# Layer-norm scalings set apart from their GpSimd rsqrt batches in a fused spectral-filter and GEGLU kernel

## The chip, the cores and the metric

The kernel runs on one core of one Trainium2 chip. The metric is the device time of one execution in microseconds (us), and the kernel before takes 195.79 us (median of three runs, 195.38 to 196.23). Engine names in the profile lines are PE (TensorE, matrix products), PEld (TensorE's weight loads), DVE (VectorE), ACT (ScalarE), POOL (GpSimd) and SP (SyncE). "Granted clock" is the share of TensorE's full clock that the throttle let through, 1.00 at best.

Executions over 1.5% slower than the fastest of the same kernel are left out of the means. Medians and ranges are over all executions.

## The reference

The input x is one batch of 2048 rows of 512 bf16 values. The output is x, plus a spectral filter of the layer-normed rows, plus a GEGLU feed-forward of the same layer-normed rows.

```python
def reference(A_x, A_w_r, A_w_i, B_x, B_w_gate, B_w_up, B_w_down):
    # A: y = irfft2(rfft2(x) * (w_r + i w_i)) over rows and features
    # B: y = (gelu(x @ w_gate) * (x @ w_up)) @ w_down, inner width 1792
    x = A_x
    xn = _layernorm(x, axis=-1)        # (x - mean) / sqrt(var + 1e-5), per row
    return x + _A_ref(xn, A_w_r, A_w_i) + _B_ref(xn, B_w_gate, B_w_up, B_w_down)
```

## The kernel before

The 2048 rows lie as 16 "columns" of 128 partitions by 512 features. Columns 0 to 3 are normalised on VectorE at the very start. Columns 4 to 15 are normalised in three groups of four:

```python
def layernorm(c0, n):                       # c0 = 4, 8, 12 with n = 4
    V = nc.vector
    ...
    for j in range(n):                      # mean and variance on VectorE
        tc.keep_in_program_order(V.bn_stats(out=stats[:, j, :], in_=x_t[:, c0 + j, :]))
        V.bn_aggr(out=mv[:, j, :], in_=stats[:, j, :])
    rsqrt(V if c0 < 4 else nc.gpsimd, rstd, mv[:, :, 1], n)   # 14 GpSimd operations, 3 Newton steps
    if c0 >= 4:
        nb = pw.tile([P, n], F32, name="nb")                  # 2 more
        nc.gpsimd.tensor_tensor(out=nb[:], in0=mv[:, :, 0], in1=rstd[:], op=ALU.mult)
        nc.gpsimd.tensor_scalar(out=nb[:], in0=nb[:], scalar1=-1.0, scalar2=None, op0=ALU.mult)
    for j in range(n):
        if c0 < 4: ...
        else:                               # the "scaling": xn = x * rstd + nb, on ScalarE
            nc.scalar.activation(out=xn[:, c0 + j, :], in_=x_t[:, c0 + j, :], func=AF.Identity,
                                 bias=nb[:, j:j + 1], scale=rstd[:, j:j + 1])
```

After that each column is transposed by a DMA (tile xnT, for the GEGLU matmuls), and VectorE folds it (tiles A and xf, for the spectral part). Four short matmul groups for each fold give PSUM tiles bp, which ScalarE copies to Bs. When all of Bs is there, the first dp matmuls can start. That is the line that divides the first third of the kernel, which this study is about, from the rest.

The GEGLU part consists of 69 blocks. One block is eight matmuls, then a GELU on ScalarE, then a multiply on VectorE:

```python
gp = ps.tile([P, w], F32, name="g_ps", tag="G", bufs=2)    # two PSUM buffers each
up = ps.tile([P, w], F32, name="u_ps", tag="U", bufs=2)
for e in range(NE): nc.tensor.matmul(gp[:], lhsT=Wg_sb..., rhs=rhs[:, e, :], ...)
for e in range(NE): nc.tensor.matmul(up[:], lhsT=Wu_sb..., rhs=rhs[:, e, :], ...)
ge = pw.tile([P, w], BF16, name="ge", bufs=3)
nc.scalar.activation(out=ge[:], in_=gp[:], func=AF.Gelu_apprx_tanh)
nc.vector.tensor_tensor(out=hT[sb, fc][:, o:o + w], in0=up[:], in1=ge[:], op=ALU.mult)
```

A list of tasks with a time each says where among the blocks the other work is issued. (The list counts up by 1.724 for each GEGLU block of 512 rows, so a unit is a bit more than half a block.)

```python
tasks = [(20, load_tables), (28, gather_tables)]
for cg in range(1, 4):
    t = 7 + 6 * (cg - 1)
    tasks.append((t, lambda cg=cg: layernorm(4 * cg, 4)))
    tasks.append((t + 6, lambda cg=cg: transposes(4 * cg, 4)))
for cg in range(4):
    t = 8 + 7 * cg
    tasks.append((t, lambda cg=cg: fold(cg)))
    for q in range(4):
        tasks.append((t + 3 + q, lambda cg=cg, q=q: pstep(cg, q)))   # bp matmuls and the Bs copy
tasks.append((36, tables_fix))
```

gather_tables issues six indirect DMAs from GpSimd.

## Time and profile before

| reading | value | view |
|---|---|---|
| time | 195.79 us, span of the profiled run 193.6 us | times, page |
| TensorE busy | 174.2 us, 90% | page, part 1 |
| TensorE idle between 17 and 64 us | 8.84 us, nearly all in three gaps | table by stretch, TensorE timeline |
| ScalarE's waits for GpSimd between 17 and 66 us | 8.9 us in three waits | waits of ScalarE |

The page of the kernel before: the busy time of each engine, and in 40 slices of the span the busy tenths of TensorE and its granted clock in tenths.

```profile
PE 174.2 (90%) x1080; PEld 93.2 (48%) x1080; DVE 116.4 (60%) x273; ACT 97.8 (51%) x181; POOL 18.8 (10%) x68
...
PE   0699975996929999999999999999999999999992
...
PEclk9999996999996999999999999999999999999999
```

TensorE is the engine at its limit. It dips in slices 6 and 7, 10 and 12 (a slice is 4.84 us), and its clock dips in slices 7 and 13. TensorE's timeline of the kernel before shows where they lie. The columns are start, busy time, engine, line, operation, tiles, shapes, count, and in brackets the idle time before and what ended it.

```profile
31.31 1.86 PE L475 MATMUL g_ps<-xnT_70,Wg_sb 128*128 128x512 bf16 x4 [3.55 <-ACT ge L481]
...
45.62 1.89 PE L475 MATMUL g_ps<-xnT_71,Wg_sb 128*128 128x512 bf16 x8 [1.56 <-ACT ge L481]
...
57.26 0.40 PE L331 MATMUL bp<-RF_t,xf 128*128 128x128 bf16 x4 [3.57 <-ACT Bs L337]
```

Each gap is ended by ScalarE: by a GELU (ge) or by a Bs copy that frees the PSUM buffer TensorE wants. ScalarE's timeline of the kernel before says why these came late.

```profile
28.07 2.93 ACT L269 ACTIVATE xn<-x_t,nb,rstd 128x512 bf16<-128x512 bf16 x4 [3.37 <-POOL nb L262]
30.90 0.36 ACT L481 ACTIVATE ge<-g_ps 128x256 bf16<-128x256 f32 x1
...
41.69 2.93 ACT L269 ACTIVATE xn<-x_t,nb,rstd 128x512 bf16<-128x512 bf16 x4 [1.42 <-POOL nb L262]
...
52.22 2.93 ACT L269 ACTIVATE xn<-x_t,nb,rstd 128x512 bf16<-128x512 bf16 x4 [4.08 <-POOL nb L262]
```

ScalarE takes its instructions in order. It stands at the first scaling with nothing to do for 3.37 us, then runs four scalings as a block of 2.93 us, and only then reaches the GELU at 30.90 that TensorE has been waiting for. What it stands waiting for is the rsqrt on GpSimd, 16 operations in a row. Part of the third of these batches, GpSimd's timeline of the kernel before:

```profile
46.77 0.23 POOL L235 TENSOR_SCALAR v<-mv 128x4 f32<-128x4 f32 x1 [5.12 <-DVE mv L257]
...
47.36 1.17 POOL L239 TENSOR_TENSOR t<-rstd 128x4 f32<-128x4 f32 x1
...
51.96 0.23 POOL L262 TENSOR_SCALAR nb<-nb 128x4 f32<-128x4 f32 x1
```

Last, the table by stretch of the kernel before. Its columns are the stretch, its length, then busy time and count of PE, PEld, DVE, ACT and POOL, the granted clock, the DMA share and GB/s.

```profile
31.30:34.40 3.10, 3.09 (x9) 1.11 (x9) 3.10 (x7) 1.99 (x4) 0.00 (x0) 0.56 0.80 130
...
57.30:61.50 4.20, 4.20 (x21) 2.16 (x22) 2.21 (x4) 1.97 (x5) 1.97 (x2) 0.59 1.14 233
61.50:134.60 73.10, 73.10 (x442) 37.17 (x439) 53.61 (x123) 56.86 (x103) 2.03 (x10) 1.00 0.23 63
```

After the first and the third gap the clock is about half (0.56, 0.59), so those two gaps cost more than their own length. From 61.5 us on TensorE is busy all the time at full clock.

### The profile page before, as it was taken

What the parts mean: (1) busy time and instruction counts of PE and PEld (TensorE: products, weight loads), DVE (VectorE), ACT (ScalarE), POOL (GpSimd) and SP (SyncE); (2) the same over time, 40 slices, a digit from 0 to 9 for tenths busy, and PEclk for the clock granted to TensorE, in tenths of its full rate; (3) what the DMA queues carried; (4) which work ended last, traced back from release to release, by engine and by line L of the source; (5) the groups of instructions that cost most, each with busy time, mean ns of one, the idle gap of its engine ahead of it and who ended that gap; (6) DMA issues with size and microseconds to landing.
All of it is one profiled execution on the core that took longest, in us unless ns stands there. A gap on an engine that the chain in (4) does not pass through costs nothing.

```text
span 193.6 us, 3075 instructions
## 1 busy us (share of the span) xinstructions
PE 174.2 (90%) x1080; PEld 93.2 (48%) x1080; DVE 116.4 (60%) x273; ACT 97.8 (51%) x181; POOL 18.8 (10%) x68
## 2 busy tenths in 40 slices
PE   0699975996929999999999999999999999999992
PEld 0688841542504544555554554545444444444440
DVE  2779915967453439868977897963726425434521
ACT  2443528377295588688898888546312112121100
POOL 0000050243774200000000000000000000000000
PEclk9999996999996999999999999999999999999999
DMA  5999914405089300220229322020021322222210
GB/s 151 326 386 387 312 48 99 68 0 108 0 216 167 110 0 0 54 51 8 54 57 327 109 56 54 3 54 0 18 67 56 108 72 77 71 81 81 68 67 28
DMA packets 22064, 19.38 MB, mean 100 GB/s; under 512 B 8289, under 2 KB 20577, under 8 KB 22049
## 3 DMA queue, kind: packets, MB, share of 16 engines
q1 hardware_dynamic: 20816, 17.22, 31.1%
q0 software_dynamic: 416, 1.32, 2.8%
q10 hardware_dynamic: 816, 0.66, 1.1%
q8 instruction: 8, 0.13, 0.3%
q14 instruction: 8, 0.06, 0.1%
HBM read 13.41 MB, written 2.10 MB: 80 GB/s over the span
## 4 chain that ended last, share of the span: by engine, by line
PE 71%; issue 7%; DVE 6%; POOL 6%; DMA 5%; ACT 3%; SPq 0%; DVEq 0%; ACTq 0%; POOLq 0%
PE y_ps L488 25%; PE u_ps L478 18%; PE g_ps L475 17%; DMA Wu_sb<-in_B_w_up_dram 4%; ACT xn L269 2%; DVE stats L256 2%; PE yp L443 2%; PE gp L428 2%; PE dp L344 2%; PE y_ps L490 2%; PE ep L356 2%; DVE hT_154 L482 2%; DMA x_t<-in_A_x_dram 2%; POOL t L239 1%; POOL rstd L248 1%
## 5 line engine op out<-in xcount | busy, mean ns | idle before, releaser
L481 ACT ACTIVATE ge<-g_ps 128x512 bf16<-128x512 f32 (+2 forms) x69 | 35.3, 520 | 22.1 <-PE g_ps L475 20.8
L478 PEld LDWEIGHTS <-Wu_sb 128*128 128x128 bf16 x276 | 26.7, 102 | 24.8 <-issue 2.6
L475 PEld LDWEIGHTS <-Wg_sb 128*128 128x128 bf16 x276 | 25.6, 101 | 24.5 <-issue 7.0
L493 DVE TENSOR_TENSOR y_sb<-y_ps,y_sb 128x512 bf16<-128x512 f32 x16 | 11.1, 692 | 30.2 <-PE y_ps L490 30.2
L449 ACT CAST yf<-yp 128x512 bf16<-128x512 f32 x16 | 9.2, 587 | 37.3 <-PE yp L443 37.3
L475 PE MATMUL g_ps<-xnT_70,Wg_sb 128*128 128x256 bf16 (+2 forms) x108 | 18.6, 297 | 4.2 <-ACT ge L481 3.6
L359 ACT CAST E<-ep 64x512 bf16<-64x512 f32 x32 | 18.5, 579 | 4.2 <-PE ep L356 3.9
L478 PE MATMUL u_ps<-xnT_70,Wu_sb 128*128 128x256 bf16 (+2 forms) x108 | 17.9, 292 | 0.4 <-DMA Wu_sb<-in_B_w_up_dram 0.3
L475 PE MATMUL g_ps<-xnT_71,Wg_sb 128*128 128x512 bf16 x56 | 14.7, 390 | 1.6 <-ACT ge L481 1.6
L478 PE MATMUL u_ps<-xnT_71,Wu_sb 128*128 128x512 bf16 x56 | 15.4, 397 | 0.0
L478 PE MATMUL u_ps<-xnT_72,Wu_sb 128*128 128x512 bf16 x56 | 14.4, 379 | 0.0
L478 PE MATMUL u_ps<-xnT_73,Wu_sb 128*128 128x512 bf16 x56 | 14.4, 379 | 0.0
L475 PE MATMUL g_ps<-xnT_73,Wg_sb 128*128 128x512 bf16 x56 | 14.4, 379 | 0.0
L475 PE MATMUL g_ps<-xnT_72,Wg_sb 128*128 128x512 bf16 x56 | 14.4, 379 | 0.0
L482 DVE TENSOR_TENSOR hT_687<-u_ps,ge 128x512 bf16<-128x512 f32 x14 | 9.5, 688 | 8.2 <-PE u_ps L478 5.5
L482 DVE TENSOR_TENSOR hT_154<-u_ps,ge 128x256 bf16<-128x256 f32 (+2 forms) x27 | 11.4, 426 | 3.4 <-PE u_ps L478 2.7
L269 ACT ACTIVATE xn<-x_t,nb,rstd 128x512 bf16<-128x512 bf16 x12 | 8.8, 801 | 8.9 <-POOL nb L262 8.9
L488 PE MATMUL y_ps<-Wd_sb,hT_1030 128*128 128x512 bf16 x56 | 12.7, 379 | 0.0
L488 PE MATMUL y_ps<-Wd_sb,hT_154 128*128 128x512 bf16 x56 | 12.7, 379 | 0.0
L488 PE MATMUL y_ps<-Wd_sb,hT_687 128*128 128x512 bf16 x56 | 12.7, 379 | 0.0
L337 ACT CAST Bs<-bp 128x512 bf16<-128x512 f32 x16 | 8.8, 582 | 2.9 <-PE bp L331 2.9
L337 ACT CAST ds<-dp 128x512 bf16<-128x512 f32 x16 | 9.2, 606 | 1.8 <-PE dp L344 1.8
(133 smaller groups left out, 223.4 us busy)
## 6 DMA issues: line engine op xcount, KB each, us to landing
y_sb<-in_A_x_dram SPq DMA_DIRECT2D x16, 128.0 KB, 2.1
out_dram<-y_sb SPq DMA_DIRECT2D x16, 128.0 KB, 1.7
Wd_sb<-in_B_w_down_dram SPq DMA_DIRECT2D x1, 1792.0 KB, 9.3
x_t<-in_A_x_dram SPq DMA_DIRECT2D x3, 512.0 KB, 12.4
Wg_sb<-in_B_w_gate_dram SPq DMA_DIRECT2D x1, 768.0 KB, 9.1
Wu_sb<-in_B_w_up_dram SPq DMA_DIRECT2D x1, 768.0 KB, 10.8
Wg_sb<-in_B_w_gate_dram SPq DMA_DIRECT2D x2, 256.0 KB, 5.3
Wg_sb<-in_B_w_gate_dram SPq DMA_DIRECT2D x1, 512.0 KB, 6.1
```

The lines of the kernel that those rows point to most:

```text
L256: tc.keep_in_program_order(V.bn_stats(out=stats[:, j, :], in_=x_t[:, c0 + j, :]))
L269: nc.scalar.activation(out=xn[:, c0 + j, :], in_=x_t[:, c0 + j, :], func=AF.Identity, bias=nb[:, j:j + 1], scale=rstd[:, j:j + 1])
L337: nc.scalar.copy(out=o, in_=i)
L344: nc.tensor.matmul(dp[:, q // 2, q % 2, :], lhsT=Bs[:, q, G].rearrange("p c r a -> p (c r a)"), rhs=FQ[q], start=(q == 0), stop=(q == 3), ...
L359: nc.scalar.copy(out=E[64 * h:64 * h + 64, r], in_=ep[64 * r:64 * r + 64])
L449: nc.scalar.copy(out=yf[:, c % 2], in_=yp[:])
L475: nc.tensor.matmul(gp[:], lhsT=Wg_sb[:, e, fc * P:(fc + 1) * P], rhs=rhs[:, e, :], start=(e == 0), stop=(e == NE - 1))
L478: nc.tensor.matmul(up[:], lhsT=Wu_sb[:, e, fc * P:(fc + 1) * P], rhs=rhs[:, e, :], start=(e == 0), stop=(e == NE - 1))
L481: nc.scalar.activation(out=ge[:], in_=gp[:], func=AF.Gelu_apprx_tanh)
L482: nc.vector.tensor_tensor(out=hT[sb, fc][:, o:o + w], in0=up[:], in1=ge[:], op=ALU.mult)
L488: nc.tensor.matmul(y_ps[:], lhsT=hT[sb, f][:, cl * P:(cl + 1) * P], rhs=Wd_sb[:, f, :], start=(f == 0), stop=False)
L493: nc.vector.tensor_tensor(out=y_sb[:], in0=y_ps[:], in1=y_sb[:], op=ALU.add)
```

## The change

The intent is that ScalarE should never stand before a scaling whose rsqrt isn't finished, and should never have four scalings in one block. The moments (mean and variance) are computed column by column, the eight last columns share one rsqrt batch, and each scaling is its own task, kept in program order, one or two per GEGLU block, about three blocks after the rsqrt is issued. Folds and short matmuls move to suit. Renamings in rsqrt and in the code of the first two columns are cut from the diff.

```diff
-    def layernorm(c0, n):
+    mv = pc.tile([P, NC, nc.vector.BN_AGGR_DIM], F32, name="mv")     # one tile for all columns
+    rstd = pc.tile([P, NC], F32, name="rstd")
+    nb = pc.tile([P, NC], F32, name="nb")
+
+    def moments(c):
         V = nc.vector
         ...
-        for j in range(n):
-            tc.keep_in_program_order(V.bn_stats(out=stats[:, j, :], in_=x_t[:, c0 + j, :]))
-            V.bn_aggr(out=mv[:, j, :], in_=stats[:, j, :])
-        rsqrt(V if c0 < 4 else nc.gpsimd, rstd, mv[:, :, 1], n)
+        tc.keep_in_program_order(V.bn_stats(out=stats[:], in_=x_t[:, c, :]))
+        V.bn_aggr(out=mv[:, c, :], in_=stats[:])
+
+    def scales(V, c0, n):
+        r, b = rstd[:, c0:c0 + n], nb[:, c0:c0 + n]
+        rsqrt(V, r, mv[:, c0:c0 + n, 1], n)
         if c0 >= 4:
             ... (nb = -mean * rstd, as before)
-        for j in range(n):
-            ...
-                nc.scalar.activation(out=xn[:, c0 + j, :], in_=x_t[:, c0 + j, :], func=AF.Identity,
-                                     bias=nb[:, j:j + 1], scale=rstd[:, j:j + 1])
+
+    def normalize(c):
+        ...
+            tc.keep_in_program_order(
+                nc.scalar.activation(out=xn[:, c, :], in_=x_t[:, c, :], func=AF.Identity,
+                                     bias=nb[:, c:c + 1], scale=rstd[:, c:c + 1]))
@@ tasks
-    for cg in range(1, 4):
-        t = 7 + 6 * (cg - 1)
-        tasks.append((t, lambda cg=cg: layernorm(4 * cg, 4)))
-        tasks.append((t + 6, lambda cg=cg: transposes(4 * cg, 4)))
+    for c0, n, t in ((4, 4, 8), (8, 8, 14)):
+        for c in range(c0, c0 + n):
+            j = c - c0
+            tasks.append((t + 0.8 * j, lambda c=c: moments(c)))
+            tasks.append((t + n + 5 + 0.9 * j, lambda c=c: (normalize(c), transposes(c, 1))))
+        tasks.append((t + n - 0.5, lambda c0=c0, n=n: scales(nc.gpsimd, c0, n)))
     for cg in range(4):
-        t = 8 + 7 * cg
+        t = (8, 21, 30.5, 34)[cg]
         tasks.append((t, lambda cg=cg: fold(cg)))
         for q in range(4):
-            tasks.append((t + 3 + q, lambda cg=cg, q=q: pstep(cg, q)))
+            tasks.append((t + (3 + q if cg < 2 else 1.5 + 0.6 * q), lambda cg=cg, q=q: pstep(cg, q)))
```

More of the change, by code (lines that the diff above doesn't have):

```diff
@@ L231, in rsqrt @@
     def rsqrt(V, y, var, n):
-        v = pw.tile([P, n], F32, name="v")
-        t = pw.tile([P, n], F32, name="t")
+        v = pc.tile([P, n], F32, name=f"v{n}")
+        t = pc.tile([P, n], F32, name=f"t{n}")
         V.tensor_scalar(out=v[:], in0=var, scalar1=EPS, scalar2=None, op0=ALU.add)
-        vi, yi = v[:].bitcast(I32), y[:].bitcast(I32)
+        vi, yi = v[:].bitcast(I32), y.bitcast(I32)
         V.tensor_scalar(out=yi, in0=vi, scalar1=-0.5, scalar2=float(0x5F3759DF), op0=ALU.mult, op1=ALU.add)
         for _ in range(3):
-            V.tensor_tensor(out=t[:], in0=y[:], in1=y[:], op=ALU.mult)
+            V.tensor_tensor(out=t[:], in0=y, in1=y, op=ALU.mult)
             if V is nc.vector:
@@ L242, in rsqrt @@
                                        op0=ALU.mult, op1=ALU.mult)
-                V.scalar_tensor_tensor(out=y[:], in0=t[:], scalar=1.5, in1=y[:],
+                V.scalar_tensor_tensor(out=y, in0=t[:], scalar=1.5, in1=y,
                                        op0=ALU.add, op1=ALU.mult)
@@ L247, in rsqrt @@
             V.tensor_scalar(out=t[:], in0=t[:], scalar1=-0.5, scalar2=1.5, op0=ALU.mult, op1=ALU.add)
-            V.tensor_tensor(out=y[:], in0=t[:], in1=y[:], op=ALU.mult)
-    def layernorm(c0, n):
-        V = nc.vector
-        stats = pw.tile([P, n, V.BN_STATS_DIM], F32, name="stats")
-        mv = pw.tile([P, n, V.BN_AGGR_DIM], F32, name="mv")
-        rstd = pw.tile([P, n], F32, name="rstd")
-        for j in range(n):
-            tc.keep_in_program_order(V.bn_stats(out=stats[:, j, :], in_=x_t[:, c0 + j, :]))
-            V.bn_aggr(out=mv[:, j, :], in_=stats[:, j, :])
-        rsqrt(V if c0 < 4 else nc.gpsimd, rstd, mv[:, :, 1], n)
-        if c0 >= 4:
-            nb = pw.tile([P, n], F32, name="nb")
-            nc.gpsimd.tensor_tensor(out=nb[:], in0=mv[:, :, 0], in1=rstd[:], op=ALU.mult)
-            nc.gpsimd.tensor_scalar(out=nb[:], in0=nb[:], scalar1=-1.0, scalar2=None, op0=ALU.mult)
-        for j in range(n):
-            if c0 < 4:
-                V.tensor_scalar(out=xn[:, c0 + j, :], in0=x_t[:, c0 + j, :],
-                                scalar1=mv[:, j, 0:1], scalar2=rstd[:, j:j + 1],
-                                op0=ALU.subtract, op1=ALU.mult)
-            else:
-                nc.scalar.activation(out=xn[:, c0 + j, :], in_=x_t[:, c0 + j, :], func=AF.Identity,
-                                     bias=nb[:, j:j + 1], scale=rstd[:, j:j + 1])
@@ new lines, in rsqrt @@
+            V.tensor_tensor(out=y, in0=t[:], in1=y, op=ALU.mult)
+    mv = pc.tile([P, NC, nc.vector.BN_AGGR_DIM], F32, name="mv")
+    rstd = pc.tile([P, NC], F32, name="rstd")
+    nb = pc.tile([P, NC], F32, name="nb")
+    def moments(c):
+        V = nc.vector
+        stats = pw.tile([P, V.BN_STATS_DIM], F32, name="stats")
+        tc.keep_in_program_order(V.bn_stats(out=stats[:], in_=x_t[:, c, :]))
[3 more added lines that the diff above has]
+        rsqrt(V, r, mv[:, c0:c0 + n, 1], n)
+        if c0 >= 4:
+            V.tensor_tensor(out=b, in0=mv[:, c0:c0 + n, 0], in1=r, op=ALU.mult)
+            V.tensor_scalar(out=b, in0=b, scalar1=-1.0, scalar2=None, op0=ALU.mult)
@@ L272, in first_columns @@
+    def normalize(c):
+        if c < 4:
+            nc.vector.tensor_scalar(out=xn[:, c, :], in0=x_t[:, c, :], scalar1=mv[:, c, 0:1],
+                                    scalar2=rstd[:, c:c + 1], op0=ALU.subtract, op1=ALU.mult)
+        else:
+            tc.keep_in_program_order(
+                nc.scalar.activation(out=xn[:, c, :], in_=x_t[:, c, :], func=AF.Identity,
+                                     bias=nb[:, c:c + 1], scale=rstd[:, c:c + 1]))
     def first_columns():
         V = nc.vector
-        stats = pw.tile([P, 2, V.BN_STATS_DIM], F32, name="stats")
@@ L276, in first_columns @@
-        mv = pw.tile([P, 2, V.BN_AGGR_DIM], F32, name="mv")
-        rstd = pw.tile([P, 2], F32, name="rstd")
+        stats = pc.tile([P, 2, V.BN_STATS_DIM], F32, name="stats2")
         def step(k, c):
@@ L497 @@
     first_columns()
-    layernorm(2, 2)
+    for c in (2, 3):
+        moments(c)
+    scales(nc.vector, 2, 2)
+    for c in (2, 3):
+        normalize(c)
     transposes(2, 2)
```

## The prediction

> **What bounds the kernel now.** TensorE. From 61.5 us to 190 us the table of engine busy time by stretch shows it busy all the time at granted clock 1.00. All its idle time after 17 us lies in three gaps (TensorE timeline): 3.55 us up to 31.3, 1.56 us up to 45.6, 3.57 us up to 57.3. Each has the same shape (timelines of GpSimd and ScalarE): the 16 GpSimd operations of a four-column rsqrt take 4.2 to 5.2 us (23.6-27.8, 37.2-41.4, 46.8-52.0), while ScalarE, which runs in order, already stands before the four scalings that wait for it and then runs them as one block of 2.93 us (28.1, 41.7, 52.2). The GELUs or Bs copies behind the block hold the PSUM buffers that TensorE needs. ScalarE idles 3.4, 1.4 and 4.1 us before the blocks.
>
> The two gaps over 3.5 us also cost clock: 0.56 granted in 31.3-34.4, 0.59 in 57.3-61.5; after the 1.56 us gap it stayed 1.00. The Trainium skill, "TensorE: Matmul & The Clock Gate", Part 1, says that about 3.4 us of idleness halves the clock, and this trace agrees. Eight 512-wide matmuls at 0.216 us need 1.73 us and took 3.07: 1.3 us lost; in the last stretch 2.39 us of matmuls took 4.2: 1.8 us. Total recoverable: 8.7 + 3.1, about 11.8 us.
>
> **What the change does.** Matmuls, GELUs and the 12 scalings (0.80 us) stay. One of three GpSimd batches goes, about 4.4 us (another becomes 8 wide, at 0.21 us an operation by the trace's 128x8 ones). More important is the order: the moments of columns 8-15 move up to the end of the first GEGLU quarter, and each scaling batch starts about one GpSimd batch (4.7 us) after its moments. In the built order of ScalarE the scalings stand one or two behind each GELU (after blocks 23, 24, 24, 25; then 29 to 33), no longer in fours. Folds and short matmuls move to suit.
>
> **Walk with the trace's durations (estimates).** Batch one again starts at 23.6, ends at 28.0; ScalarE reaches its first scaling at 29.2: no wait. Last scaling 33.7, last transpose (1.25 us issue, 2.5 to landing) about 36.5; TensorE wants it at 36.2: 0.4 us stall. Batch two: 33.8 to 38.5, stretched up to 2 us where VectorE's folds run beside it (before, one GpSimd operation took 1.17 us beside them instead of 0.20); ScalarE wants it at 40.6: 0 to 0.5. From there ScalarE is nearly saturated until the last scaling at 51.4; the folds follow it closely, so the short matmuls stall 0.5 us (columns 8-11) and 0.3 us (12-15), and the first dp matmuls wait about 1 us for the Bs copies. New stalls together 2 to 2.5 us, none long enough to cost clock. Before, the GEGLU block behind the first dp ended at 69.2; after, at about 59. From there the order is the same and TensorE-bound, so the gain stays in the total.
>
> **Prediction: 185.8 us, 184.0 to 189.5**; faster by over 2% 0.94, within 2% 0.05, slower 0.01.
>
> **Signs.** TensorE idle 17-62 us falls from 8.7 to 1.5-3 us; granted clock near 1.00 from 17 us on; ScalarE's waits for GpSimd vanish; no ScalarE block of 2.93 us; tail from the first dp on unchanged.
>
> **What would make it wrong.** A scaling that still reaches ScalarE's head before batch two is done; late transposes at the second quarter; folds pinned before GEGLU multiplies on VectorE; the gathers crowding the transposes' DMA.

## The result

The changed kernel takes 185.48 us (median of four runs, 185.20 to 185.55), beside 195.58 us for the kernel before in the same rounds. The ratio is 0.948, with a 95% interval of 0.945 to 0.951. All ratios here are the mean time of one kernel's fast runs over that of the other's of the same rounds, so they are not quite the ratio of the medians that are quoted.

The same lines of the page, for the changed kernel:

```profile
PE 172.2 (94%) x1080; PEld 92.7 (50%) x1080; DVE 116.1 (63%) x273; ACT 97.8 (53%) x181; POOL 17.2 (9%) x52
...
PE   0699999899899999999999999999999999999991
...
PEclk9999999999999999999999999999999999999998
```

The dips are gone, of TensorE as of its clock (all but the last slice). TensorE's timeline of the changed kernel has two stalls left between 17 and 64 us, both short:

```profile
36.72 1.02 PE L477 MATMUL g_ps<-xnT,Wg_sb 128*128 128x512 bf16 x4 [0.55 <-DMA xnT<-xn]
...
48.96 0.40 PE L333 MATMUL bp<-RF_t,xf 128*128 128x128 bf16 x4 [0.60 <-DVE xf L323]
```

The first waits for a transposing DMA, the second for a fold. TensorE's whole idle time there, read from the table by stretch as 47.00 us less its busy time, is 1.19 us (45.81 busy), where it was 8.84 us (38.16 busy). ScalarE's waits between 17 and 66 us, first the kernel before, then the changed one (columns: engine, waiting tile and line, what it waited for, us in total, times, longest us):

```profile
ACT xn L269 <- POOL nb L262: 8.9, 3, 4.1
```

```profile
ACT xn L273 <- POOL nb L265: 0.4, 1, 0.4
```

8.9 us have become 0.4 us. On ScalarE's timeline of the changed kernel no scalings stand in blocks of four. The first of each batch:

```profile
28.97 0.81 ACT L273 ACTIVATE xn<-x_t,nb,rstd 128x512 bf16<-128x512 bf16 x1
...
42.00 0.81 ACT L273 ACTIVATE xn<-x_t,nb,rstd 128x512 bf16<-128x512 bf16 x1 [0.37 <-POOL nb L265]
```

The eight-wide batch on GpSimd took 5.8 us, from 36.16 to 41.97. GpSimd's timeline of the changed kernel:

```profile
36.16 0.60 POOL L235 TENSOR_SCALAR v<-mv 128x8 f32<-128x8 f32 x1 [7.22 <-DVE mv L258]
...
37.40 0.20 POOL L239 TENSOR_TENSOR t<-rstd 128x8 f32<-128x8 f32 x1
...
38.59 0.52 POOL L248 TENSOR_TENSOR rstd<-t,rstd 128x8 f32<-128x8 f32 x1
...
41.73 0.24 POOL L265 TENSOR_SCALAR nb<-nb 128x8 f32<-128x8 f32 x1
```

And VectorE's timeline of the changed kernel beside it:

```profile
36.56 0.68 DVE L321 TENSOR_TENSOR A<-xn 128x1024 bf16<-128x1024 bf16 x1
37.17 0.69 DVE L484 TENSOR_TENSOR hT<-u_ps,ge 128x512 bf16<-128x512 f32 x1
...
38.37 0.68 DVE L325 TENSOR_TENSOR xf<-A 128x1024 bf16<-128x1024 bf16 x1
```

Four of the sixteen GpSimd operations took 0.48 to 0.60 us instead of 0.20. They are those that meet a fold (tiles A and xf, both inputs in SBUF), and not those that meet a GEGLU multiply (hT, which reads one input from PSUM), such as the one at 37.40. The Trainium skill, "SBUF — State Buffer", section "Who interferes with whom", says that VectorE and GpSimd share a port pair as an exclusive lock, and that a tensor_tensor with both inputs in SBUF contends with GpSimd's reads. This trace agrees: each of the four ends about 0.1 us after the end of the fold that it met.

The time can be followed along the kernel. The first dp matmul starts at 56.24 us instead of 66.86 (10.6 us earlier). The addition of the last output on VectorE starts at 179.82 instead of 190.01 (10.2 us), and the span ends 9.8 us earlier. So nearly everything that was gained in the first third stayed gained. The half microsecond that went missing behind was not followed up.

### The profile page after: what moved, and what is told of

Read it like the earlier page. It is cut to its first block, busy times and chain, and to the rows that moved or that the text cites. A ratio compares the mean times of both kernels' runs of the same rounds, so it can differ in the third digit from the quotient of the medians.

```text
span 183.8 us, 3059 instructions
## 1 busy us (share of the span) xinstructions
PE 172.2 (94%) x1080; PEld 92.7 (50%) x1080; DVE 116.1 (63%) x273; ACT 97.8 (53%) x181; POOL 17.2 (9%) x52
## 4 chain that ended last, share of the span: by engine, by line
PE 83%; DVE 4%; DMA 3%; POOL 3%; issue 3%; ACT 2%; ACTq 0%
PE y_ps L490 26%; PE g_ps L477 22%; PE u_ps L480 22%; DMA Wu_sb<-in_B_w_up_dram 3%; PE dp L346 2%; PE ep L358 2%; PE yp L445 2%; PE gp L430 2%; PE y_ps L492 2%; DVE hT L484 2%; PE bp L333 2%; ACT xn L273 1%; ACT ge L483 1%; DVE stats L257 1%; PE tp L306 1%
## 5 line engine op out<-in xcount | busy, mean ns | idle before, releaser
L477 PE MATMUL g_ps<-xnT,Wg_sb 128*128 128x512 bf16 (+2 forms) x276 | 62.3, 347 | 1.1 <-DMA xnT<-xn 0.5
L480 PE MATMUL u_ps<-xnT,Wu_sb 128*128 128x512 bf16 (+2 forms) x276 | 60.9, 344 | 0.1
L490 PE MATMUL y_ps<-Wd_sb,hT 128*128 128x512 bf16 x224 | 51.0, 379 | 0.0
L484 DVE TENSOR_TENSOR hT<-u_ps,ge 128x512 bf16<-128x512 f32 (+2 forms) x69 | 40.1, 583 | 15.0 <-PE u_ps L480 7.5
L490 PEld LDWEIGHTS <-hT 128*128 128x128 bf16 x224 | 21.3, 98 | 23.1
L339 ACT CAST Gs<-gp 128x512 bf16<-128x512 f32 x16 | 8.6, 591 | 1.4 <-PE gp L430 1.4
L257 DVE BATCH_NORM_STATS2 stats<-x_t 128x6 f32<-128x512 bf16 x14 | 9.2, 667 | 0.0
L492 PE MATMUL y_ps<-yt,RI_t 128*128 128x512 bf16 x16 | 6.1, 379 | 0.0
L346 PE MATMUL dp<-CT,Bs 128*128 128x128 bf16 x64 | 6.0, 219 | 0.0
L333 PE MATMUL bp<-RF_t,xf 128*128 128x128 bf16 x64 | 5.4, 219 | 0.6 <-DVE xf L323 0.6
## 6 DMA issues: line engine op xcount, KB each, us to landing
Wu_sb<-in_B_w_up_dram SPq DMA_DIRECT2D x1, 768.0 KB, 10.6
```

Of the source, the lines that this page charges most:

```text
L257: tc.keep_in_program_order(V.bn_stats(out=stats[:], in_=x_t[:, c, :]))
L339: nc.scalar.copy(out=o, in_=i)
L346: nc.tensor.matmul(dp[:, q // 2, q % 2, :], lhsT=Bs[:, q, G].rearrange("p c r a -> p (c r a)"), rhs=FQ[q], start=(q == 0), stop=(q == 3), ...
L477: nc.tensor.matmul(gp[:], lhsT=Wg_sb[:, e, fc * P:(fc + 1) * P], rhs=rhs[:, e, :], start=(e == 0), stop=(e == NE - 1))
L480: nc.tensor.matmul(up[:], lhsT=Wu_sb[:, e, fc * P:(fc + 1) * P], rhs=rhs[:, e, :], start=(e == 0), stop=(e == NE - 1))
L490: nc.tensor.matmul(y_ps[:], lhsT=hT[sb, f][:, cl * P:(cl + 1) * P], rhs=Wd_sb[:, f, :], start=(f == 0), stop=False)
```

## The experiments

Three explanations can be given for the gain. They are called A, B and C in the expectations:

- A, distance: the scalings reach ScalarE's head after their rsqrt is done, so ScalarE no longer stands idle.
- B, fewer batches: one of three GpSimd batches is gone.
- C, splitting: there is no longer a block of four scalings (2.93 us) in front of the GELUs.

The first four kernels ran on one chip, where the kernel before took 195.59 us (194.67 to 196.48, seven runs). The other eight ran on another chip, where it took 195.48 and 195.37 us.

### Distance alone: d_delay_only

This is the kernel before with its three batches of four and its blocks of four scalings. Only the scalings are issued later (kept in program order), with the transposes; folds and short matmuls move as far as that needs.

```diff
-        for j in range(n):
-            ... the four scalings, right after the rsqrt
+    def scalings(cg):                      # the same four, in program order
+        ...
-        tasks.append((t + 6, lambda cg=cg: transposes(4 * cg, 4)))
+        tasks.append(((0, 17, 24, 29)[cg], lambda cg=cg: (scalings(cg), transposes(4 * cg, 4))))
     for cg in range(4):
-        t = 8 + 7 * cg
+        t = (8, 21, 28, 34)[cg]
         ...
-            tasks.append((t + 3 + q, lambda cg=cg, q=q: pstep(cg, q)))
+            tasks.append((t + (3 + q if cg < 3 else 1.5 + 0.6 * q), lambda cg=cg, q=q: pstep(cg, q)))
```

> Kernel before with one thing changed: the four ScalarE scalings of a batch are issued one GpSimd batch later (three batches of 4, scalings still in blocks of four, moments as before; folds and short matmuls moved behind them as they must). Theory A, the gain is the distance between a batch and its scalings: no wait of ScalarE for GpSimd over 0.5 us, no TensorE gap over 1.5 us, 185 to 187.5 us. Rival B, the gain is the GpSimd batch that went: 191 us or more. Rival C, the gain is that the scalings no longer stand in a block of 2.93 us: 190 us or more.

Measured: 185.51 us (185.42 to 185.63), ratio 0.948, 95% 0.944 to 0.952. That is the ratio of the whole change. ScalarE's timeline of this kernel, and then its TensorE timeline:

```profile
29.13 2.92 ACT L276 ACTIVATE xn<-x_t,nb,rstd 128x512 bf16<-128x512 bf16 x4
...
36.04 2.92 ACT L276 ACTIVATE xn<-x_t,nb,rstd 128x512 bf16<-128x512 bf16 x4
...
45.29 2.93 ACT L276 ACTIVATE xn<-x_t,nb,rstd 128x512 bf16<-128x512 bf16 x4 [2.66 <-POOL nb L262]
```

```profile
36.60 1.02 PE L482 MATMUL g_ps<-xnT,Wg_sb 128*128 128x512 bf16 x4 [0.23 <-DMA xnT<-xn]
...
48.75 1.02 PE L482 MATMUL g_ps<-xnT,Wg_sb 128*128 128x512 bf16 x4 [1.99 <-ACT ge L488]
```

Two blocks of 2.92 us came with no wait before them, and no GELU gap on TensorE followed: the stall at 36.60 is a transposing DMA's. The third block came 2.66 us before its rsqrt was done and cost a gap of 1.99 us. So a block by itself is harmless; a block with a wait before it is not. Two signs that A expected (no wait over 0.5 us, no gap over 1.5 us) thus failed for the third block, though the time came as expected. B and C fall as explanations of the gain, and A stands. No run moves the folds and short matmuls alone, so their share in this version isn't shown; b_first_batch_no_distance below moves scalings and transposes alone.

### Three batches instead of two: a_three_batches

This is the changed kernel with the eight-wide batch split into two of four.

```diff
-        tasks.append((t + n - 0.5, lambda c0=c0, n=n: scales(nc.gpsimd, c0, n)))
+        for h in range(c0, c0 + n, 4):
+            tasks.append((t + 0.8 * (h - c0 + 3) + 0.1 if h + 4 < c0 + n else t + n - 0.5,
+                          lambda h=h: scales(nc.gpsimd, h, 4)))
```

> Changed kernel with its 8-column rsqrt batch cut into two of 4 (48 GpSimd operations again instead of 32), everything else at the same places. A: 185.0 to 185.8 us, since the added 4.5 us of GpSimd stay behind ScalarE's other work. B: 4 us longer, about 189.5 us.

Measured: 186.13 us (185.88 to 186.32), ratio 0.951, 95% 0.947 to 0.955. It is 0.3 us above what A expected and 3.4 us below what B expected. ScalarE waits nowhere for GpSimd. The 0.3 us are not the batches' doing as far as the trace shows: TensorE's timeline has one gap more than expected, 1.07 us at 54.41, which is of the kind found further below (late releases). B falls a second time.

### Blocks of four scalings: c_blocks_of_four

This is the changed kernel with its scalings in blocks of four again, at the time of the first of each four.

```diff
-            tasks.append((t + n + 5 + 0.9 * j, lambda c=c: (normalize(c), transposes(c, 1))))
+            tasks.append((t + n + 5 + 3.6 * (j // 4), lambda c=c: (normalize(c), transposes(c, 1))))
```

> Changed kernel with the scalings again in blocks of four, at the delayed time of the first of each four. A: a block of 2.93 us that waits for nothing fits between the GELUs of two buffers, TensorE idles at most 1.5 us in all, 185 to 187 us. C: the block itself holds up the GELUs, gaps of about 3 us come back, 190 us or more.

Measured: 187.85 us (187.60 to 188.44), ratio 0.960, 95% 0.956 to 0.965. That lies above what A expected (185 to 187) and below what C expected (190 or more). ScalarE's timeline of this kernel, then its TensorE timeline, then its table by stretch:

```profile
28.90 2.93 ACT L273 ACTIVATE xn<-x_t,nb,rstd 128x512 bf16<-128x512 bf16 x4
...
42.92 2.93 ACT L273 ACTIVATE xn<-x_t,nb,rstd 128x512 bf16<-128x512 bf16 x4 [1.63 <-POOL nb L265]
```

```profile
46.86 1.90 PE L477 MATMUL g_ps<-xnT,Wg_sb 128*128 128x512 bf16 x5 [2.52 <-ACT ge L483]
```

```profile
43.88:47.29 3.41, 0.89 (x5) 0.29 (x3) 1.41 (x3) 3.41 (x7) 2.50 (x4) 1.00 0.65 166
47.29:50.71 3.42, 3.42 (x10) 1.21 (x9) 2.90 (x5) 3.30 (x6) 2.59 (x3) 0.50 1.08 209
```

The first block, which had no wait, again caused no gap. The second waited 1.63 us for the eight-wide batch and caused a gap of 2.52 us, the only one. The clock then halved for 3.42 us, in which TensorE was busy all the time: a loss of about 1.7 us by this trace (half of 3.42). The times show less: one of the four executions ran at clock 1.00 throughout and took 187.60 us, where the other three (clock 0.986 to 0.991) took 187.84 to 188.44. The prediction's reading, that it takes about 3.4 us of idleness, doesn't foresee this half-clock stretch. So a block matters where its batch is late. Whether single scalings would have made less of the same wait isn't shown: in the changed kernel the wait at this place was only 0.37 us.

This table also tells how the clock is judged. The windows are 3.41 us long and lie on a fixed grid. Narrowing the stretches of this table finds the two half-clock stretches of the kernel before at 30.65 to 34.06 and 57.95 to 61.36, which is 27.30 us or 8 steps of 3.41 us apart. The table by stretch of the kernel before, laid on that grid:

```profile
27.23:30.65 3.42, 0.53 (x6) 0.29 (x5) 0.00 (x0) 2.58 (x4) 0.63 (x3) 1.00 0.13 27
30.65:34.06 3.41, 2.75 (x7) 0.99 (x7) 3.03 (x7) 2.64 (x6) 0.00 (x0) 0.50 0.59 124
...
44.30:47.71 3.41, 2.09 (x10) 0.97 (x10) 3.06 (x7) 2.51 (x6) 0.77 (x3) 1.00 0.41 83
54.53:57.95 3.42, 0.69 (x6) 0.47 (x7) 2.74 (x5) 3.42 (x8) 2.51 (x4) 1.00 0.92 274
57.95:61.36 3.41, 3.41 (x15) 1.59 (x13) 1.42 (x3) 1.18 (x4) 1.61 (x2) 0.50 1.23 226
```

Windows in which TensorE was busy for 0.53 and 0.69 us (and 0.89 us in c_blocks_of_four) were followed by a window at clock 0.50. The window that holds most of the 1.56 us gap, busy for 2.09 us, was not. The Trainium skill, "TensorE: Matmul & The Clock Gate", Part 1, names a free-running window of 3413 ns, and these traces agree with that length. What they add is that the window needn't be idle throughout: a gap of 2.52 us was enough where it lay inside one window. Other traces narrow the limit, with the grid laid from the drop to half clock at the end of each kernel: a window with 1.39 us of work was followed by half clock (a_three_batches, 179.43 to 182.84), windows with 1.34 (l_best_early, 35.99 to 39.41) and 1.43 us (b_first_batch_no_distance, 58.66 to 62.07) were not. So the limit in these traces lies near 1.4 us of work in 3.41. It can't be had more exactly, since the ends of matmuls are modelled.

### The first batch without distance: b_first_batch_no_distance

This is the changed kernel, with the first four scalings (and their transposes) issued 5.4 units of the task list (about three blocks) earlier, so that they reach ScalarE before their rsqrt is done.

```diff
-            tasks.append((t + n + 5 + 0.9 * j, lambda c=c: (normalize(c), transposes(c, 1))))
+            tasks.append((t + n + (5 if c0 > 4 else -0.4) + 0.9 * j, lambda c=c: (normalize(c), transposes(c, 1))))
```

> Changed kernel with the scalings of columns 4 to 7 alone moved back right behind their GpSimd batch, still split (two, one, one). A: ScalarE waits about 4.4 us for GpSimd before the first, TensorE gets one gap of about 3 us near 29 us, total 2.4 to 4.5 us longer than the changed kernel (188 to 190 us). B and C: unchanged at 185.5 us, since batches and splitting are kept.

Measured: 192.96 us (192.45 to 193.92), ratio 0.987, 95% 0.982 to 0.993. The direction was right, but the loss was 7.5 us against the changed kernel's 185.48 where 2.5 to 4.5 us had been expected. ScalarE's timeline of this kernel, then its TensorE, VectorE and GpSimd timelines:

```profile
29.47 1.52 ACT L273 ACTIVATE xn<-x_t,nb,rstd 128x512 bf16<-128x512 bf16 x2 [3.61 <-POOL nb L265]
```

```profile
32.70 1.02 PE L477 MATMUL g_ps<-xnT,Wg_sb 128*128 128x512 bf16 x4 [2.93 <-ACT ge L483]
...
60.64 1.24 PE L477 MATMUL g_ps<-xnT,Wg_sb 128*128 128x512 bf16 x5 [2.05 <-ACT ge L483]
```

```profile
32.68 0.69 DVE L484 TENSOR_TENSOR hT<-u_ps,ge 128x512 bf16<-128x512 f32 x1 [6.28 <-ACT ge L483]
```

```profile
42.34 0.24 POOL L235 TENSOR_SCALAR v<-mv 128x8 f32<-128x8 f32 x1 [12.90 <-DVE mv L258]
```

The wait of 3.61 us makes a gap of 2.93 us on TensorE, and the scalings here stand alone or in pairs, so it takes no block to make a gap. The rest is a knock-on that the expectation missed. The late GELU holds up a GEGLU multiply on VectorE (6.28 us of idleness before 32.68), the moments of columns 8 to 15 stand in order behind it, and so the second batch starts at 42.34 instead of 36.16. ScalarE then waits 1.91 us for that one too, and TensorE's idle time between 17 and 64 us comes to 7.14 us. The last gap, 2.05 us at 60.64, has another cause, the late releases found below (a Bs copy waited 2.35 us, until 56.65, for a bp group that had ended at 54.91), so about 2 us of the loss are not the knock-on's. The clock was 1.00 throughout: a gap of 2.93 us cost none here where one of 2.52 us did in c_blocks_of_four. That fits the fixed grid. This trace's record of the clock has a drop to half at 191.78 us, just behind the last instruction; 47 steps of 3.413 us before it, a line of the grid lies at 31.35, inside the gap (29.77 to 32.70). The table by stretch has 1.83 us of work in the window before that line and 2.07 in the one behind. The other three executions had clock 0.982 to 0.991, so there some gap did cost clock.

### The clock loss taken away: e_before_warm

This is the kernel before with sixteen more matmuls, which compute one u_ps tile four times again (the accumulation starts anew each time, so the result is the same). They fill the third gap, so that TensorE doesn't idle there.

```diff
-        for e in range(NE):
-            nc.tensor.matmul(up[:], lhsT=Wu_sb[:, e, fc * P:(fc + 1) * P], rhs=rhs[:, e, :],
-                             start=(e == 0), stop=(e == NE - 1))
+        again = 4 if (c0, n, fc) in ((4, 4, 4),) else 0
+        for k in range(again + 1):
+            for e in range(NE):
+                nc.tensor.matmul(up[:], ...)        # as before
```

> Kernel before, with the four u matmuls of the GEGLU block just ahead of its third gap repeated four times (16 matmuls, 3.46 us, same values written again; the order on every engine is otherwise that of before). They fill the idle stretch 53.7 to 57.3 us, so TensorE arrives warm at the end of it. If the clock loss behind the gap is a real part of the sum (1.8 us by the trace of before), the kernel is faster by 1.3 to 2.0 us, about 193.8 us, with granted clock 1.00 in the 4 us behind the gap, although it does more work. If something else limits that stretch anyway (the folds on VectorE, the Bs copies on ScalarE), it stays at 195.6 us.

Measured: 193.79 us (193.42 to 194.71) beside 195.48, ratio 0.995, 95% 0.989 to 1.000. By the times alone a gain isn't certain, since the interval reaches 1. The trace is clearer. The table by stretch of this kernel, for the stretch that had clock 0.59 before:

```profile
57.30:61.50 4.20, 4.15 (x30) 2.23 (x29) 1.90 (x4) 2.03 (x5) 2.12 (x3) 1.00 1.40 240
```

The clock is 1.00, and the first dp matmul starts at 65.07 instead of 66.86, 1.8 us earlier, although TensorE computes more. That is the 1.8 us that the prediction had put down to the clock at the third gap.

### A slower batch: f_more_newton

This is the changed kernel with a fourth Newton step in each GpSimd rsqrt, so four more operations in each batch. It tells how much room the scalings have.

```diff
-        for _ in range(3):
+        for _ in range(3 if V is nc.vector else 4):
```

> Changed kernel with one more Newton step in the GpSimd rsqrt: four more operations, 1.1 us, on each of its two batches; the order is the same on all engines. By the trace the distance has 0.0 us of slack in the first batch and -0.4 us in the second. If GpSimd latency bounds it there, both batches push ScalarE by about 1.1 us: waits of ScalarE for GpSimd of about 1.1 and 1.5 us, total 1.2 to 2.3 us longer than the changed kernel. If ScalarE's own queue is what bounds it, under 0.5 us longer.

Measured: 188.49 us (188.35 to 189.16, four runs), ratio 0.968, 95% 0.961 to 0.975, where the changed kernel itself took 187.41 (after_again, below). The loss of 1.1 us lies just below the 1.2 to 2.3 us expected, and no interval was taken between these two. ScalarE now waits for GpSimd 1.04 and 0.65 us (1.1 and 1.5 had been expected) instead of 0.4 in all. So there is next to no room left: at the first batch the four added operations come through nearly whole. The second wait adds little, since the first has already pushed ScalarE back.

### A version to beat both: g_best

The readings so far say what a better kernel needs: the distance of d_delay_only, a little more of it for the third block, and a shorter batch. Two Newton steps instead of three on GpSimd still gave results within the tolerance.

```diff
 (against d_delay_only)
-        for _ in range(3):
+        for _ in range(3 if V is nc.vector else 2):
-        tasks.append(((0, 17, 24, 29)[cg], lambda cg=cg: (scalings(cg), transposes(4 * cg, 4))))
+        tasks.append(((0, 17, 24, 30.5)[cg], lambda cg=cg: (scalings(cg), transposes(4 * cg, 4))))
```

> The delay alone (three batches, blocks of four) with the third block one GEGLU block later and two Newton steps instead of three on GpSimd. In the delay-only run TensorE still had one gap of 2.0 us, from the third block waiting 2.7 us for GpSimd. Distance as the cause: that wait and that gap go, TensorE idles under 0.7 us from 17 to 60 us, 183.2 to 184.2 us, the fastest so far. Otherwise 185.5 us.

Measured: 184.91 us (184.68 to 185.31, six runs), ratio 0.948, 95% 0.943 to 0.954. ScalarE's waits for GpSimd and the gap of 1.99 us are gone as expected. TensorE's idle time from 17 to 60 us is 1.72 us where under 0.7 had been expected, and the time missed the expectation by 0.7 us.

### The changed kernel again: after_again and after_third

Both are the changed kernel, letter for letter, on the second chip.

> The changed kernel again, on the chip of the other runs of this group, as their yardstick: 185.2 to 185.8 us.

> The changed kernel a third time, as the yardstick of this group. It has shown 185.5 us on one chip and 187.4 us on another. In the slower trace the semaphore updates of TensorE arrive up to 1.8 us after the matmuls that post them, and bunched, between 47 and 51 us, while the gathers' data move (44 to 52 us); in the faster trace none is over 0.4 us late. Either value may come; where it is the slower one, the trace should show such late updates between 44 and 53 us, and nowhere else.

Measured: 187.41 us (187.19 to 188.82) and 187.36 us (187.20 to 190.02, of which one slow), ratios 0.963 (95% 0.958 to 0.969) and 0.958 (0.953 to 0.962). That is 1.9 us slower than in its first runs, twice, with the kernel before at its old time. The first repeat missed its expectation. The granted clock of both profiled runs is 0.998, and nine of the twelve runs lie between 187.2 and 187.7 us. TensorE's and ScalarE's timelines of after_again:

```profile
48.77 0.40 PE L333 MATMUL bp<-RF_t,xf 128*128 128x128 bf16 x4 [0.62 <-DVE xf L323]
...
55.03 0.81 PE L477 MATMUL g_ps<-xnT,Wg_sb 128*128 128x512 bf16 x3 [1.74 <-ACT ge L483]
```

```profile
51.03 0.59 ACT L339 CAST Bs<-bp 128x512 bf16<-128x512 f32 x1 [2.47 <-PE g_ps L477]
```

The same place on ScalarE's timeline of the first run of the changed kernel:

```profile
49.39 0.58 ACT L339 CAST Bs<-bp 128x512 bf16<-128x512 f32 x1 [0.65 <-PE bp L333]
```

This Bs copy waits 2.47 us instead of 0.65, though the bp group that it reads ends at about the same time: 49.17 us in after_again (48.77 + 0.40), 49.35 in the first run. The copy's waiting time is put down to a g_ps matmul, but that is only the record nearest to its start. The order of the instructions tells more: the Bs copies follow in the order of the bp groups, so each copy can be set beside the end of its group. These are, in all fourteen traces, the copies that began more than one microsecond after their group's end although ScalarE stood idle, with the window in which the data of the six indirect DMAs was moving:

```
run                        bp group's end -> Bs copy's start, us      indirect DMAs' data us
before                     none                                       54.2 - 63.3
changed kernel, first run  none                                       44.0 - 52.6
d_delay_only               51.08 -> 52.76                             47.3 - 56.8
a_three_batches            50.10 -> 52.09                             45.2 - 55.0
c_blocks_of_four           none                                       44.9 - 54.0
b_first_batch_no_distance  54.91 -> 56.65                             49.6 - 58.0
e_before_warm              59.61 -> 61.17                             54.1 - 63.0
f_more_newton              50.49 -> 52.58                             45.2 - 53.7
g_best                     48.71 -> 51.03   48.93 -> 53.16            46.2 - 55.8
after_again                49.17 -> 51.03                             43.8 - 52.1
after_third                49.74 -> 51.52                             44.4 - 52.6
n_plain_loads              none (no indirect DMA)                     -
g_best_again               48.77 -> 50.37   48.99 -> 52.73            46.2 - 56.6
l_best_early               41.38 -> 43.22                             36.4 - 43.4
```

All of them lie within the time in which the indirect DMAs' data moves. The trace also records when TensorE's semaphore updates came; each update releases the readers of a PSUM tile. (A single update that is missing there is no sign of a late release: in the kernel before, none is recorded for 1.53 us after the bp group that ends at 57.66, and yet its copy starts at 57.91.) In after_again the bp group ended at 49.17 us, its update came at 51.01, and the Bs copy started at 51.03. Four more updates followed bunched, at 51.08 to 51.37. TensorE itself went on with matmuls meanwhile. The Trainium skill, "Perfetto Trace Analysis", section "Tensor Engine Instruction (MATMUL, LD_WEIGHTS)", says that a matmul's end is an estimate and that the update is pushed when PSUM has acknowledged all bytes. So the trace can't say whether the write to PSUM or the update behind it was late. It says that the release was. It isn't the second chip alone: three of the first four experiments, on the other chip, have such releases too. The record doesn't name the chip of the changed kernel's first runs.

A late release at 47 to 52 us falls on the stretch in which the changed kernel's ScalarE has no slack left, and it costs a gap of 1.74 us at 55.03.

### The cause of the late releases: n_plain_loads

The changed kernel with the six indirect DMAs replaced by six plain ones of the same bytes, issued by SyncE. They load other rows, so the result is wrong (relative error 0.030).

```diff
         def gather(out, rows, col):
-            tc.keep_in_program_order(nc.gpsimd.indirect_dma_start(
-                out=out, out_offset=None, in_=rows,
-                in_offset=bass.IndirectOffsetOnAxis(ap=idx_t[:, col:col + 1], axis=0)))
+            lo = (0, 1024, 0)[col]
+            tc.keep_in_program_order(nc.sync.dma_start(out=out, in_=rows[lo:lo + P, :]))
```

> Changed kernel with the six GpSimd gathers of table rows replaced by six plain loads of as many bytes, issued by SyncE at about the same time (wrong rows, so a wrong result on purpose); all other engines keep their order. If the gathers themselves (GpSimd-issued, indirect) hold up the semaphore updates, no update is over 0.4 us late and the time is 185.0 to 185.6 us even where the changed kernel shows 187.4. If it is the DMA traffic as such, late updates stay, and the time is that of the changed kernel within 0.5 us.

Measured: 185.27 us (185.09 to 185.73), ratio 0.948, on the chip where the changed kernel took 187.4. No copy is held up, and the gap at 55 us is gone, although the plain loads move their data in the same stretch (45.9 to 51.9 us). The Bs copy of above, on ScalarE's timeline of this kernel:

```profile
49.56 0.59 ACT L338 CAST Bs<-bp 128x512 bf16<-128x512 f32 x1 [0.64 <-PE bp L332]
```

So the late releases come with the indirect DMAs from GpSimd, not with the traffic as such. What in them does it stays open. The Trainium skill, "DMA: Bandwidth & Descriptors", section "SWDGE vs HWDGE vs iDMA", says that GpSimd's DMAs have their descriptors computed by GpSimd's own cores, and SyncE's by dedicated hardware. This experiment changes that, the indirection and the exact time of the transfers at once. The indirect DMAs are not enough by themselves either: the kernel before, the first run of the changed kernel and c_blocks_of_four have them and no held-up copy.

### Gathers earlier: g_best_again and l_best_early

g_best_again is g_best, letter for letter. l_best_early moves the gathers to between the second and the third GpSimd batch, away from the stretch without slack; its other edits only keep GpSimd's order.

```diff
-    tasks = [(20, load_tables), (28, gather_tables)]
+    tasks = [(13.1, load_tables), (13.2, gather_tables)]
-    tasks.append((36, tables_fix))
+    tasks.append((34.5, tables_fix))        # its operations, and the last of each batch, in program order
```

> The best version so far again: 184.6 to 185.4 us, faster than the changed kernel of this group by 0.5 us (if that shows 185.5) to 2.5 us (if it shows 187.4), because it has slack where the changed kernel has none.

> The best version with the six gathers moved on GpSimd from behind the third rsqrt batch to between the second and the third (about 33.5 to 41 us). If the gathers hold up the semaphore updates, late updates move to 35 to 44 us, where ScalarE has slack, and the time falls to 183.3 to 184.4 us; if the third batch is pushed past 45.5 us by them, it stays at 184.9 us or worse.

Measured: g_best_again 184.82 us (184.66 to 185.48), ratio 0.946, 95% 0.942 to 0.950. l_best_early 185.55 us (184.94 to 185.73), ratio 0.948. The late release moved along, to 41 to 43 us, but TensorE's timeline of l_best_early has a new stall:

```profile
38.61 1.02 PE L482 MATMUL g_ps<-xnT,Wg_sb 128*128 128x512 bf16 x4 [2.08 <-DMA xnT<-xn]
```

The transposing DMAs for the second GEGLU quarter now share their time with the gathers, and TensorE waits 2.08 us for them (0.46 us in g_best). The third batch ends at 46.31 us, past the 45.5 beyond which no gain had been expected. The move gains nothing. g_best stays the best version: on this chip it takes 184.8 to 184.9 us where the changed kernel takes 187.4. Its first release is late by 2.3 us as well, but its last scalings are done at 47.2 us instead of 54.0 (after_again), so ScalarE can make the delay good. Against the changed kernel's first runs (185.48) the lead is only 0.6 us, and against d_delay_only the two ratios to the kernel before don't differ (0.946 and 0.948 against 0.948).

## Why the prediction was right

The prediction said 185.8 us, 184.0 to 189.5; measured were 185.48 us. Its mechanism held as well, with some luck: the first scaling was to have 1.2 us to spare behind its batch and had 0.04 us, because the batch began at 24.46 instead of 23.6 us.

| step of the prediction | predicted | measured |
|---|---|---|
| batch one ends, first scaling starts | 28.0, 29.2 us | 28.93, 28.97 us, no wait, no margin |
| stall for the last transpose | 0.4 us at 36.2 | 0.55 us at 36.72 |
| batch two | 33.8 to 38.5, stretched up to 2 us | 36.16 to 41.97 |
| ScalarE's wait for batch two | 0 to 0.5 us | 0.37 us |
| short matmuls' stall, columns 8 to 11 | 0.5 us | 0.60 us |
| short matmuls' stall, columns 12 to 15, and first dp matmuls | 0.3 and about 1 us | none of 0.15 us or more |
| new stalls together | 2 to 2.5 us | 1.19 us, all idle time 17 to 64 |
| block behind the first dp ends | about 59 us (69.2 before) | 58.65 us |

- **The three gaps and what makes them.** d_delay_only confirms it: moving nothing but the scalings (with the transposes, folds and short matmuls behind them) gives the whole ratio, 0.948. The prediction named the order as "more important" than the batch that goes, and a_three_batches shows the batch to be worth nothing by itself. The prediction didn't weigh the wait against the block of four; d_delay_only and c_blocks_of_four show that the wait is what counts, and that a block without one costs nothing.
- **The clock loss of 3.1 us.** It was right in size for the trace that it was read from. Laid on the grid it is 1.37 us (half of the 2.75 us busy in the first half-clock window) and 1.71 us (half of 3.41), and e_before_warm got the second back, 1.8 us by its trace. But the grid falls differently in each execution, and over all executions the clock was worth less: the fast ones of the kernel before took 194.11 us on average at clock 0.991 (3 executions), 195.19 at 0.982 (10) and 195.95 at 0.974 (13; one more, at 0.987, took 193.48). One half-clock window in 194 us is a step of 0.009 in the clock, so by these times a window costs about 0.9 us, not 1.3 to 1.8 (an estimate). The reason given, a gap of about 3.4 us, was too simple: a gap of 2.52 us cost clock, and one of 2.93 us didn't.
- **The mis-sized terms.** Batch two began 2.4 us later than thought. It took 5.8 us, within the 4.7 to 6.7 us allowed, with four operations of 0.48 to 0.60 us beside folds where "0.21 us" had been given for one alone. The wait of the dp matmuls, "about 1 us", didn't come. The stalls were thus overstated by about 1 us, and 0.4 us of that were lost again between the first dp matmul and the last addition. The total is 0.3 us off.
- **The signs.** TensorE's idle time fell to 1.19 us (1.5 to 3 had been named), the clock is 1.00 from 17 us to the last slices, ScalarE's waits for GpSimd fell from 8.9 to 0.4 us, and no block of 2.93 us is left.
- **What the prediction missed.** It named the gathers as a risk, for crowding the transposes' DMA. What they really brought was late releases of PSUM tiles, 1.9 us for the whole kernel; the profiled one of its first runs had none. That the first runs, by their times, were free of them is luck; even so, 187.4 us lies inside the range. Crowded transposes appeared only where an experiment moved the gathers onto them (l_best_early, 2.08 us).

## What to carry to other kernels

An engine that works in order should meet an instruction only after its input is surely done: distance between producer and consumer was worth 10 us here. Fewer batches added 0.7 us at most, and splitting the scalings wasn't needed where the distance was kept. Price a TensorE gap with the clock in mind: where it leaves less than about 1.4 us of work in one fixed 3.4 us window, the next window ran at half clock here. A schedule without slack on one engine is fragile, so run it again, on another chip, before trusting one time, and prefer the version that finishes its waiting work early, even at an equal median.

## What the Trainium skill lacked or had wrong

- "TensorE: Matmul & The Clock Gate", Part 1: the free-running window of 3413 ns is right (two half-clock stretches of 3.41 us, 8 steps apart), but "≥1 idle window" is too strict. Windows with 0.53 to 1.39 us of work out of 3.41 were followed by a window at half clock, those with 1.34, 1.43 and 2.09 us weren't. The page lacks this limit, near 1.4 us here, and its advice of no gaps over about 3 us doesn't cover the 2.52 us gap that halved the clock of the next window.
- No page has it that the readers of TensorE's results can be released 1.6 to 2.3 us after the modelled end of the matmul (4.2 us for one copy) while indirect DMAs from GpSimd are under way; with plain SyncE loads none was. "Perfetto Trace Analysis" says only that the end is an estimate.
- "SBUF — State Buffer", section "Who interferes with whom", says that DMA never contends with a compute engine and that TensorE never waits on anyone. It speaks of SBUF's ports, and no run here shows it wrong: TensorE itself went on. But it has no warning that the readers of TensorE's results can be held up with GpSimd's indirect DMAs (2.47 us before one Bs copy instead of 0.65), which cost the kernel about 2 us.
- The same section is right that two-input VectorE operations hold up GpSimd, but gives no size for short operations: here 0.48 to 0.60 us instead of 0.20, and 1.17 us in one case before the change.
